# A state-space scan with routed experts: experts 4 to 7 in one wide pass, the first unit's scores first, and a copy moved to VectorE

## The chip, the cores and the metric

The kernel runs on one core of a Trainium2 chip. The time is device microseconds (us) of one launch, and a version is told by the median of several runs; the profile is of one further execution, whose own time is given beside its span. Engines are called by the names of the profile: PE is TensorE's matmul, PEld its weight load, DVE is VectorE, ACT ScalarE, POOL GpSimd, SP SyncE (here it only issues transfers).

## The reference

Two blocks, one after the other. The first is a state-space scan over 4 x 8 heads and 768 positions, in chunks; what it leaves is an array of 3072 tokens by 256. The second sends each token to one of eight experts, the one with the largest logit, and weighs what the expert gives by the softmax probability:

```python
y_intra = einsum('bhij,bhjd->bhid', CB * L, xc)
y_inter = einsum('bhin,bhnd->bhid', Cc, state) * decay_to_i
state = decay_full * state + sum(Bx)
...
logits = x @ w_gate                       # 3072 x 8
expert_idx = argmax(logits, axis=1)
for e in range(8):
    h = maximum(x[mask_e] @ w1[e], 0.0)   # 256 -> 1024
    out[mask_e] = gate_w[mask_e] * (h @ w2[e])
```

The inputs are fixed, and so is the routing: worked out from the reference, experts 0 to 7 get 372, 343, 418, 417, 336, 365, 415 and 406 tokens.

## The kernel before

**Scan.** Twelve steps `d` (L752 to L855), each for two units of 128 positions. For a unit `n`, `masked_C` (L254) makes two masked copies of C, `scores` (L274) multiplies them with B on PE into the accumulator `g`, `weigh` (L280) masks `g` into `M` on DVE, `scaled_x` (L264) divides x by its decay, `y_own` and `y_old` make the output on PE, ACT copies it (`turned`), and `rows` (L345) turns it and makes the logits. `totals` and `take_totals` (L243, L248) hand the decay over a whole chunk to the next one: `et` by DVE and `ew` by ACT, both read from the same PSUM bank that `rows` writes. Ahead of the loop (L731 to L746) stands the first pair of units by itself, with matmuls on zeros (`idle`) that keep PE at work.

**Places.** A token's place in the table `x_hbm` (an area of 3584 rows for each expert, in HBM) is its rank within its expert. GpSimd writes each unit's rows there by indirect transfers (`place`, L430). When all are placed, `over` (L447) works out where each expert's tokens end, and `empty_rest(e)` (L473) writes 128 empty rows behind the last token of expert `e`.

**Experts.** Everything is float32. `jobs` (L476) is the list of passes: sixteen before the change, (0, e) for the first 256 rows of each expert, then (1, e) for the rows from 256 on. A pass is
- `m_load(i)` (L479): SP issues four transfers of x into `xb`, one of logits and token numbers into `lt`, and, for the second pass of an even expert, two into `lh`.
- `m_xT(i)` (L515): DVE transposes `xb` to `xT`. For second passes it does so for two experts, i and i+1, and then for both `lt` and the `lh` runs `gates` (L498): three DVE operations, an exponential on ACT, three DVE operations.
- `m_h(i)` (L554): for each of eight blocks `f` two matmuls (`up`, L547) into one of four accumulators `h_ps`, then a relu by ACT into `hT`. After each block it calls `between(f)` of the loop at L869, which hands out other work. At f = 4 that is, in this order: weights of expert i+2 (`load_w`), `over` (i = 1), two `empty_rest` (i = 1 to 4), `m_load(i + 3)`, the switch number of a pair (`number_of`), and `m_xT(i + 1)`. So ACT gets the exponentials of `m_xT(i + 1)` ahead of its relus for f = 5, 6 and 7.
- `m_y(i)` (L581): for each tile of 128 rows eight matmuls into one of two accumulators `y_ps`, a scaling (`put`: by ACT, and by DVE from job 7 on) and an indirect transfer to the output on POOL's queue.

Second passes go in pairs of experts (`m_pair`, L615): a switch over 17 sizes, 128 to 192 rows in steps of 4, picks the code that fits the larger of the two counts; rows over 128 of both experts share one tile (`m_half`, L592). After pair k (L916) come `m_load` for pair k+2, `m_xT` for pair k+1, and `m_y` for both experts.

**Order.** The whole block is in `tc.manual_schedule()`: each engine and each queue runs its instructions in the order in which the code emits them, and waits are put in where data or buffers demand it. Reads and writes of `x_hbm` on SP's and POOL's queues wait for each other: a `m_load` for the `empty_rest` before it, an `empty_rest` for the `m_load` before it; only the indirect writes among themselves don't.

Of the kernel before, what the change touches and what calls it, by code (L numbers as in the profile page):

```python
# [9 lines left out]
FP32 = mybir.dt.float32  # L10
# [29 lines left out]
SLACK, FEW = 64, 64  # L40
NR = N + 512
EW = 3
# [5 lines left out]
def ssd_then_moe(ctx, tc, xs_in, ae_in, wgx, w_gate, w1, w2, gx, gb, gc, ga, out):  # L48
# [42 lines left out]
    steps = route.tile([1, len(SIZES) - 1], FP32, name="steps")  # L91
# [69 lines left out]
    def empty_consts():  # L161
        nc.gpsimd.memset(zrows, 0.0)
        none = sm.tile([128, 1], I32, name="none")
        nc.gpsimd.iota(none, pattern=[[0, 1]], base=N, channel_multiplier=0)
        nc.gpsimd.tensor_copy(zrows[:, TOK:TOK + 1].bitcast(I32), none)
        at_i = sm.tile([128, E], I32, name="at_i")
        nc.gpsimd.iota(at_i, pattern=[[NR, E]], base=0, channel_multiplier=1)
        nc.gpsimd.tensor_copy(at_r, at_i)
        steps_i = sm.tile([1, len(SIZES) - 1], I32, name="steps_i")
        nc.gpsimd.iota(steps_i, pattern=[[SIZES[1] - SIZES[0], len(SIZES) - 1]], base=P1 + SIZES[0],  # L170
                       channel_multiplier=0)
        nc.gpsimd.tensor_copy(steps, steps_i)
# [67 lines left out]
    def lasts(w):  # L240
        nc.vector.tensor_scalar(out=last[:, w], in0=here, scalar1=cum[:, w, CH - 1:CH], scalar2=None, op0=ALU.mult)  # L241
# [6 lines left out]
    def take_totals(w):  # L248
        p = r_ps[:, 1, 416:428]
        nc.vector.tensor_tensor(out=et[:, 12 * w:12 * w + 12], in0=bc(p[:, :, None], [128, 12, 2]),  # L250
                                in1=bc(par[:, None, :], [128, 12, 2]), op=ALU.mult)
        nc.scalar.copy(ew[:, 12 * w:12 * w + 12], p)  # L252

    def masked_C(n, dve=False):  # L254
        t = wk.tile([128, 2, CH], FP32, name="cm", bufs=4)
        for u in range(2):
            if dve:
                nc.vector.tensor_scalar(out=t[:, u], in0=st[n]["CT"], scalar1=par[:, u:u + 1], scalar2=None,
                                        op0=ALU.mult)
            else:  # L260
                nc.scalar.mul(t[:, u], st[n]["CT"], par[:, u:u + 1])  # L261
        st[n]["cm"] = t
# [184 lines left out]
    def over():  # L447
# [10 lines left out]
        nc.vector.tensor_tensor(out=over_, in0=bc(most[:, :, None], sh), in1=bc(steps[:, None, :], sh), op=ALU.is_gt)  # L458
# [17 lines left out]
    jobs = [(0, e) for e in range(E)] + [(1, e) for e in range(E)]  # L476
    ex = [dict() for _ in jobs]

    def m_load(i, engs=(nc.sync,)):  # L479

        p, e = jobs[i]
        r0, n = e * NR + P1 * p, (P1, P2)[p]
        xb = mo.tile([128, P1 // 32 * 64], FP32, name="xb", bufs=4)
        for c in range(4):
            engs[c % len(engs)].dma_start(out=xb[32 * c:32 * c + 32, 0:2 * n].rearrange("p (r z) -> p r z", z=64),
                              in_=x_hbm[r0:r0 + n, 64 * c:64 * c + 64].rearrange("(r j) z -> j r z", j=32))
        ex[i]["xb"] = xb[:, 0:2 * n].rearrange("p (r i k) -> p k r i", k=KT, i=32)
        lt = mo.tile([128, 2, MID], FP32, name="lt", bufs=7)[:, 0:2 - p]
        nc.sync.dma_start(out=lt, in_=x_hbm[r0:r0 + 128 * (2 - p), DM:W].rearrange("(t p) w -> p t w", p=128))
        ex[i]["lt"] = lt  # L490
        if p and e % 2 == 0:
            lh = mo.tile([128, 1, MID], FP32, name="lh", bufs=3)
            for u in range(2):
                q = r0 + u * NR + 128
                nc.sync.dma_start(out=lh[64 * u:64 * u + 64, 0], in_=x_hbm[q:q + 64, DM:W])
            ex[i]["lh"] = ex[i + 1]["lh"] = lh

    def gates(mid, n):  # L498

        sh = [128, n, E]  # L500
        l = mo.tile([128, 2, E], FP32, name="t_l", bufs=2)[:, 0:n]
        logits(l, mid)
        mx = mo.tile([128, 2], FP32, name="t_mx", bufs=2)[:, 0:n]
        nc.vector.tensor_reduce(mx, l, axis=AX, op=ALU.max)
        sub = mo.tile([128, 2, E], FP32, name="t_sub", bufs=2)[:, 0:n]
        nc.vector.tensor_tensor(out=sub, in0=l, in1=bc(mx[:, :, None], sh), op=ALU.subtract)
        nc.scalar.activation(sub, sub, func=ACT.Exp)  # L507
        se = mo.tile([128, 2], FP32, name="t_se", bufs=2)[:, 0:n]
        nc.vector.tensor_reduce(se, sub, axis=AX, op=ALU.add)  # L509
        nc.vector.tensor_scalar(out=se, in0=se, scalar1=1e-9, scalar2=None, op0=ALU.add)  # L510
        gt = mo.tile([128, 2], FP32, name="t_gt", bufs=8)[:, 0:n]
        nc.vector.reciprocal(gt, se)
        return gt

    def m_xT(i):  # L515
        p, e = jobs[i]
        n = (P1, P2)[p]
        for j in range(i, i + 1 + p):
            ex[j]["xT"] = mo.tile([128, KT, P1], FP32, name="xT", bufs=4)
            nc.vector.transpose(ex[j]["xT"][:, :, 0:n].rearrange("p k (r j) -> p k r j", j=32), ex[j]["xb"])  # L520
        if p:
            for j in range(i, i + 2):
                ex[j]["g"] = gates(ex[j]["lt"], 1)
# [3 lines left out]
    hT_all = [mo.tile([128, FT, P1], FP32, name=f"hT{k}") for k in range(3)]  # L527
# [26 lines left out]
    def m_h(i, pp, between):  # L554
        p, e = jobs[i]
        n = (P1, P2)[p]
# [24 lines left out]
    def m_y(i, pp, then=None):  # L581
        e = jobs[i][1]
        for t in range(2 - jobs[i][0]):
# [4 lines left out]
            put(p, ex[i]["lt"][:, t], ex[i]["g"][:, t:t + 1], i >= E - 1)  # L588
# [3 lines left out]
    def m_half(i, n, yo):  # L592
        e = jobs[i][1]
# [3 lines left out]
        p = y_next()  # L597
        for f in range(FT):
            for u in range(2):
                nc.tensor.matmul(p[64 * u:64 * u + n, :], lhsT=ex[i + u]["hT"][:, f, 128:128 + n],  # L600
                                 rhs=w_sb[e + u][1][:, f * DM:f * DM + DM], start=(f == 0), stop=(f == FT - 1))
        nc.scalar.mul(yo, p, ex[i]["gh"][:, 0:1])  # L602
# [12 lines left out]
    def m_pair(i, pp):  # L615

        e = jobs[i][1]
# [4 lines left out]
        for c in tc.Switch(chosen(e // 2), len(SIZES), hint=f"pair{e // 2}"):  # L622
            turn_no[:] = at
            n = SIZES[c]
# [4 lines left out]
            m_half(i, max(0, n - 128), yo)  # L629
# [84 lines left out]
    with tc.manual_schedule():  # L714
# [19 lines left out]
        idle(14)  # L734
        decays(0)
        masked_C(0)
        masked_C(1, dve=True)
        p0 = turn_decays(0)
        inverse(0, p0, 0, 4)
        for n in range(2):  # L740
            scores(n)
        rep_consts()
        scaled_x(0, nc.vector)
        scaled_x(1, nc.gpsimd)
        lasts(0)
# [6 lines left out]
        for d in range(ND):  # L752
# [37 lines left out]
            if d == 0:  # L790
                idle(3)
# [6 lines left out]
            weigh(2 * d)  # L798
            weigh(2 * d + 1)
            if d == 0:  # L800
                take_totals(0)
                inverse(0, p0, 4, 12)
# [37 lines left out]
            if d == 1:  # L840
# [3 lines left out]
                lasts(1)  # L844
# [16 lines left out]
        for e in range(EW, E):  # L861
            w_sb.append([w2pool.tile([128, KT * F], FP32, name=f"w{u + 1}_{e}") for u in range(2)])
        left = list(range(R0[LAST], NU))
# [5 lines left out]
        for i in range(E):  # L869
            def between(f):  # L870
# [21 lines left out]
                if EW <= i + 2 < E:  # L892
# [4 lines left out]
                if 1 <= i <= 4:  # L897
# [3 lines left out]
                if i == E - 1:  # L901
                    m_load(i + 4)
                if 2 <= i < 2 + E // 2:
                    number_of(i - 2)
                if i == E - 2:
# [6 lines left out]
            if i < E - 1:  # L912
                m_y(i, pp, (lambda: more_places(2)) if i == 0 else None)
        tc.switch_hint(chosen(0), len(SIZES), "pair0")
        m_y(E - 1, pp)
        for k in range(E // 2):  # L916
            i = E + 2 * k
            m_pair(i, pp)
            if k + 1 < E // 2:
                tc.switch_hint(chosen(k + 1), len(SIZES), f"pair{k + 1}")  # L920
                for u in range(4, 6):
                    if i + u < len(jobs):
                        m_load(i + u)
                m_xT(i + 2)
            m_y(i, pp)
            m_y(i + 1, pp)
    with tc.If(more[0] > 0):
# [65 lines left out]
```

## Time and profile before

| what | value |
|---|---|
| median of 3 runs | 248.17 us (247.75 to 251.34) |
| the profiled execution: its time | 247.47 us |
| the profiled execution: its span | 245.8 us |
| granted PE clock | 1.0 throughout |
| ACT busy | 92.7 us (38%) |
| POOL busy | 82.8 us (34%) |
| scan: PE, from the start to | 60.56 us |
| first passes, jobs 0 to 7, from / to | 60.56 / 172.95 us |
| second passes, from / to the last matmul's end | 172.95 / 240.9 us |

The span is the time from the first to the last instruction that the profiler recorded; 1.67 us lie around it. A float32 matmul stands in the records as two, so `up` of one expert makes 32 records of PE and a tile of `m_y` 16; these records are called passes of PE below. Busy times of PE are modelled at their ends, so the starts of successive stages say more than means.

### The profile page before, as it was taken

What the parts mean: (1) busy time and instruction counts of PE and PEld (TensorE: products, weight loads), DVE (VectorE), ACT (ScalarE), POOL (GpSimd) and SP (SyncE); (2) the same over time, 40 slices, a digit from 0 to 9 for tenths busy, and PEclk for the clock granted to TensorE, in tenths of its full rate; (3) what the DMA queues carried; (4) which work ended last, traced back from release to release, by engine and by line L of the source; (5) the groups of instructions that cost most, each with busy time, mean ns of one, the idle gap of its engine ahead of it and who ended that gap; (6) DMA issues with size and microseconds to landing.
All of it is one profiled execution on the core that took longest, in us unless ns stands there. A gap on an engine that the chain in (4) does not pass through costs nothing. (4 is left out here: it accounts for less than half of the span.)

```text
span 245.8 us, 5525 instructions
## 1 busy us (share of the span) xinstructions
PE 237.3 (97%) x2021; PEld 201.3 (82%) x2021; DVE 88.5 (36%) x279; ACT 92.7 (38%) x312; POOL 82.8 (34%) x144
## 2 busy tenths in 40 slices
PE   8889899999999999999999999999999999999992
PEld 5567778777888888888888888888999969989781
DVE  4699879998520222020201102052316007040000
ACT  4656768981322224141422324131432502614200
POOL 2484688880038506060413330111113012013031
PEclk9999999999999999999999999999999999999999
DMA  6999979965932278696867779454303100001001
GB/s 174 327 328 323 332 250 302 291 263 102 274 141 97 112 144 274 189 256 217 235 243 213 272 168 311 87 99 82 73 13 68 32 15 29 27 4 40 3 16 45
DMA packets 36407, 39.75 MB, mean 162 GB/s; under 512 B 21947, under 2 KB 23806, under 8 KB 36352
## 3 DMA queue, kind: packets, MB, share of 16 engines
q1 hardware_dynamic: 32816, 30.24, 43.2%
q0 software_dynamic: 2880, 8.66, 9.3%
q8 instruction: 27, 0.44, 0.7%
q10 hardware_dynamic: 656, 0.18, 0.3%
q14 instruction: 28, 0.23, 0.3%
HBM read 29.72 MB, written 9.86 MB: 161 GB/s over the span
## 5 line engine op out<-in xcount | busy, mean ns | idle before, releaser
L551 PE MATMUL h_ps<-xT,w 128*128 128x256 f32 (+3 forms) x512 | 90.0, 334 | 0.3 <-ACT hT L628 0.3
L551 PEld LDWEIGHTS h_ps<-xT,w 128*128 128x128 f32 x512 | 80.8, 190 | 7.6 <-ACT hT L628 0.7
L586 PE MATMUL y_ps<-w,hT 128*128 128x256 f32 x384 | 85.1, 380 | 0.0
L586 PEld LDWEIGHTS y_ps<-w,hT 128*128 128x128 f32 x384 | 72.6, 190 | 10.5 <-issue 0.8
L564 POOL DMA_INDIRECT out_dram<-yo,lt x24 | 23.8, 991 | 58.1 <-DVE yo L571 31.3
L509 DVE TENSOR_REDUCE t_se<-t_sub 128x1 f32<-128x8 f32 (+1 forms) x20 | 3.3, 165 | 102.8 <-ACT t_sub L507 102.8
L560 ACT ACTIVATE hT<-h_ps 128x256 f32<-128x256 f32 x64 | 24.4, 384 | 29.4 <-PE h_ps L551 28.9
L282 DVE TENSOR_TENSOR M<-g,mask 128x1024 f32<-128x1024 f32 x24 | 28.2, 1218 | 3.8 <-PE g L277 3.6
L628 ACT ACTIVATE hT<-h_ps 128x128 f32<-128x128 f32 (+2 forms) x64 | 18.0, 292 | 24.1 <-PE h_ps L551 24.1
L421 POOL DMA_INDIRECT x_hbm<-rows,pos x24 | 23.9, 994 | 9.3 <-DVE pos L408 5.3
L573 ACT ACTIVATE yo<-y_ps,t_gt 128x256 f32<-128x256 f32 x14 | 6.6, 474 | 43.2 <-PE y_ps L586 43.2
L421 POOL DMA_INDIRECT x_hbm<-zrows,rest x8 | 7.7, 962 | 35.4 <-DMA lt<-x_hbm 24.9
L335 PE MATMUL y<-M,xp 128*32 128x128 f32 x384 | 15.3, 277 | 1.6 <-DVE M L282 1.3
L347 PEld LDWEIGHTS r<-turn,yT 128*128 128x128 f32 x88 | 12.2, 189 | 4.4 <-ACT yT L340 3.0
L261 ACT ACTIVATE cm<-xs_n,par 128x128 f32<-128x128 f32 x46 | 15.1, 419 | 1.5 <-DMA xs_n<-in_xs_dram 1.5
L347 PE MATMUL r<-turn,yT 128*128 128x160 f32 x88 | 14.9, 312 | 0.7 <-ACT ew L252 0.7
L564 POOL DMA_INDIRECT out_dram<-yh,lh x4 | 3.9, 983 | 33.1 <-ACT yh L602 21.2
L277 PE MATMUL g<-cm,xs_n 32*128 32x256 f32 x192 | 15.0, 423 | 0.0
L271 POOL TENSOR_TENSOR xp<-xs_n,Ei 128x256 f32<-128x256 f32 x20 | 12.1, 617 | 6.8 <-DVE last L241 3.6
L571 DVE TENSOR_SCALAR yo<-y_ps,t_gt 128x256 f32<-128x256 f32 x10 | 4.7, 483 | 24.2 <-PE y_ps L586 24.2
L340 ACT COPY yT<-y 128x512 f32<-128x512 f32 x12 | 7.0, 586 | 16.1 <-PE y L335 14.2
L520 DVE STREAM_TRANSPOSE xT<-xb 128x512 f32<-128x512 f32 (+1 forms) x16 | 9.8, 632 | 8.6 <-DMA xb<-x_hbm 7.1
(123 smaller groups left out, 156.2 us busy)
## 6 DMA issues: line engine op xcount, KB each, us to landing
w<-in_w_dram SPq DMA_DIRECT2D x64, 256.0 KB, 5.8
xs_n<-in_xs_dram SPq DMA_DIRECT2D x20, 320.0 KB, 5.8
xb<-x_hbm SPq DMA_DIRECT2D x30, 64.0 KB, 2.3
xb<-x_hbm SPq DMA_DIRECT2D x32, 48.0 KB, 2.4
xs_n<-in_xs_dram SPq DMA_DIRECT2D x4, 192.0 KB, 3.6
x_hbm<-zrows SPq DMA_DIRECT2D x1, 672.0 KB
lt<-x_hbm SPq DMA_DIRECT2D x8, 80.0 KB, 2.7
xs_n<-in_xs_dram SPq DMA_DIRECT2D x4, 128.0 KB, 2.3
```

What stands on the lines that cost most here:

```text
L261: nc.scalar.mul(t[:, u], st[n]["CT"], par[:, u:u + 1])
L271: eng.tensor_tensor(out=t, in0=st[n]["x"].rearrange("p (h d) -> p h d", d=D), in1=bc(Ei[:, n, :, None], [128, NH, D]), op=ALU.mult)
L277: nc.tensor.matmul(g_ps[:, q, n % 2], lhsT=st[n]["BT"][r], rhs=st[n]["cm"][r].rearrange("p u i -> p (u i)"), start=True, stop=True)
L282: nc.vector.tensor_tensor(out=t, in0=g_ps[:, :, n % 2].rearrange("p q (u i) -> p q u i", u=2), in1=bc(mask[:, None, None, :], [128, 4, 2, ...
L335: nc.tensor.matmul(y_ps[o:o + D, h // 4, CH * s:CH * s + CH], lhsT=st[n]["xp"][:, D * h:D * h + D], rhs=st[n]["M"][:, h], start=first, sto ...
L347: nc.tensor.matmul((to[s] if to else r_ps[:, s])[:, 256 * t:256 * t + 160], lhsT=sd[d]["yT"][:, t, CH * s:CH * s + CH], rhs=turn[:, t].rea ...
L421: s_ = nc.gpsimd.indirect_dma_start(out=x_hbm[:, :], out_offset=bass.IndirectOffsetOnAxis(ap=at, axis=0), in_=row, in_offset=None)
L551: nc.tensor.matmul(p[:, 0:n], lhsT=w[:, c:c + 128], rhs=xT[:, t, 0:n], start=(t == 0), stop=(t == KT - 1))
L560: nc.scalar.activation(ex[i]["hT"][:, f, 0:n], q, func=ACT.Relu)
L564: return nc.gpsimd.indirect_dma_start(out=out[:, :], out_offset=bass.IndirectOffsetOnAxis(ap=tok, axis=0), in_=yo[:, :], in_offset=None, b ...
L586: nc.tensor.matmul(p, lhsT=ex[i]["hT"][:, f, 128 * t:128 * t + 128], rhs=w_sb[e][1][:, f * DM:f * DM + DM], start=(f == 0), stop=(f == FT ...
L628: nc.scalar.activation(ex[i + u]["hT"][:, f, 0:n], q, func=ACT.Relu)
```

## The change

1. **Start of the scan.** The first unit's masked C is made half by ACT and half by DVE, the second unit's wholly by ACT; the first unit's `scores` stand ahead of the turning of the decays on PE, its `weigh` ahead of the decays' inverse on DVE; three `idle` matmuls move in between the two units' scores. `lasts(0)` goes from DVE to GpSimd.
2. **Totals.** `take_totals` makes `ew` by DVE instead of ACT, and at d = 0 stands behind the second inverse.
3. **Experts.** Twelve jobs: (0, e) and (1, e) for experts 0 to 3, then (2, e) for experts 4 to 7, which takes all rows of an expert at once: 320 to 448 in steps of 8, three tiles of 128 in `m_y`, rows over 384 in `m_half`. The loop over first passes has 4 rounds, not 8. Three `hT` of 256 columns become two of 448, whose columns 320 to 383 are set to zero by GpSimd during the scan. Weights of experts 6 and 7 go into the buffers of experts 0 and 1 after pair 0. `empty_rest` of experts 0 to 5 stay in rounds 1 to 3, those of 6 and 7 go behind pair 0. `over` compares with two lists of sizes.

```diff
+HE = E // 2
+PASS = ((0, P1, 2), (P1, P2, 1), (0, P1 + P2, 3))
+WSIZES = list(range(P1 + FEW, P1 + P2 + 1, 8))
...
+        for hT in hT_all:
+            nc.gpsimd.memset(hT[:, :, WSIZES[0]:P1 + 128], 0.0)
...
-    def lasts(w):
-        nc.vector.tensor_scalar(out=last[:, w], in0=here, scalar1=cum[:, w, CH - 1:CH], scalar2=None, op0=ALU.mult)
+    def lasts(w, eng):
+        eng.tensor_scalar(out=last[:, w], in0=here, scalar1=cum[:, w, CH - 1:CH], scalar2=None, op0=ALU.mult)
...
-        nc.scalar.copy(ew[:, 12 * w:12 * w + 12], p)
+        nc.vector.tensor_copy(ew[:, 12 * w:12 * w + 12], p)
...
-    jobs = [(0, e) for e in range(E)] + [(1, e) for e in range(E)]
+    jobs = [(p, e) for p in range(2) for e in range(HE)] + [(2, e) for e in range(HE, E)]
...
-        r0, n = e * NR + P1 * p, (P1, P2)[p]
-        xb = mo.tile([128, P1 // 32 * 64], FP32, name="xb", bufs=4)
+        at, n, tiles = PASS[p]
+        r0 = e * NR + at
+        xb = mo.tile([128, (n if p == 2 else P1) // 32 * 64], FP32, name="xw" if p == 2 else "xb", bufs=2 if p == 2 else 4)
...
-        for j in range(i, i + 1 + p):
-            ex[j]["xT"] = mo.tile([128, KT, P1], FP32, name="xT", bufs=4)
+        for j in range(i, i + (2 if p else 1)):
+            ex[j]["xT"] = (mo.tile([128, KT, n], FP32, name="xTw", bufs=2) if p == 2 else
+                           mo.tile([128, KT, P1], FP32, name="xT", bufs=4))
...
-    hT_all = [mo.tile([128, FT, P1], FP32, name=f"hT{k}") for k in range(3)]
+    hT_all = [mo.tile([128, FT, P1 + P2], FP32, name=f"hT{k}") for k in range(2)]
...
-            n = SIZES[c]
+            n = (SIZES, WSIZES)[p - 1][c]
...
+        masked_C(0, (None, nc.vector))
+        masked_C(1)
         decays(0)
-        masked_C(0)
-        masked_C(1, dve=True)
+        scores(0)
         p0 = turn_decays(0)
+        idle(3, y_ps[:, 1, 256:512])
+        weigh(0)
+        scores(1)
         inverse(0, p0, 0, 4)
-        for n in range(2):
-            scores(n)
-        rep_consts()
         scaled_x(0, nc.vector)
         scaled_x(1, nc.gpsimd)
-        lasts(0)
+        rep_consts()
+        lasts(0, nc.gpsimd)
...
-        for i in range(E):
+        for i in range(HE):
...
-                if EW <= i + 2 < E:
+                if EW <= i + 2 < E - 2:
                     for k in range(8):
                         load_w(i + 2, *divmod(k, 4))
                 if i == 1:
                     over()
-                if 1 <= i <= 4:
+                if 1 <= i:
                     for e in range(2 * i - 2, 2 * i):
                         empty_rest(e)
                 m_load(i + 3)
-                if i == E - 1:
+                if i == HE - 1:
                     m_load(i + 4)
-                if 2 <= i < 2 + E // 2:
-                    number_of(i - 2)
+                if i >= 2:
+                    for k in range(2):
+                        number_of(2 * i - 4 + k)
...
                 m_xT(i + 1)
...
         for k in range(E // 2):
-            i = E + 2 * k
+            i = HE + 2 * k
             m_pair(i, pp)
             if k + 1 < E // 2:
...
+                m_xT(i + 2)
+                if k == 0:
+                    for e in range(E - 2, E):
+                        empty_rest(e)
                 for u in range(4, 6):
                     if i + u < len(jobs):
                         m_load(i + u)
-                m_xT(i + 2)
             m_y(i, pp)
             m_y(i + 1, pp)
+            if k == 0:
+                for e in range(E - 2, E):
+                    for j in range(8):
+                        load_w(e, *divmod(j, 4))
```

## The prediction

> **What bounds the kernel now.** I read the page's busy shares first, then PE's timeline, then the queues that feed it. The page's first lines:
>
> ```profile
> PE 237.3 (97%) x2021; PEld 201.3 (82%) x2021; DVE 88.5 (36%) x279; ACT 92.7 (38%) x312; POOL 82.8 (34%) x144
> ...
> L586 PE MATMUL y_ps<-w,hT 128*128 128x256 f32 x384 | 85.1, 380 | 0.0
> ```
>
> PE is busy 97%, and `m_y` waited 0.0 us: from 60.56 us on PE is the bound. Its timeline (start, length, what) shows how closely the stages follow each other. Round 3 of the first passes:
>
> ```profile
> 103.88 7.07 PE L551 MATMUL h_ps<-xT,w 128*128 128x256 f32 x32
> 110.79 7.07 PE L586 MATMUL y_ps<-w,hT 128*128 128x256 f32 x32
> 117.70 7.07 PE L551 MATMUL h_ps<-xT,w 128*128 128x256 f32 x32
> ```
>
> Start to start is 6.91 us for 32 passes, 215.9 ns each. But that no transfer is late holds only for this order of jobs. SP's timeline has the loads of jobs 4 and 5 (four `xb`, one `lt`) and between them the weights of expert 4:
>
> ```profile
> 100.86 1.81 SPq L485 DMA_DIRECT2D xb<-x_hbm  x4
> 102.71 0.45 SPq L489 DMA_DIRECT2D lt<-x_hbm  x1
> 103.21 3.81 SPq L204 DMA_DIRECT2D w<-in_w_dram  x8
> 114.01 1.81 SPq L485 DMA_DIRECT2D xb<-x_hbm  x4
> 115.86 0.45 SPq L489 DMA_DIRECT2D lt<-x_hbm  x1
> ```
>
> and POOL's has the empty rows that they wait for:
>
> ```profile
> 105.77 0.96 POOL L421 DMA_INDIRECT x_hbm<-zrows,rest  x1 [7.46 <-DMA lt<-x_hbm]
> ...
> 107.04 0.96 POOL L421 DMA_INDIRECT x_hbm<-zrows,rest  x1 [0.23 <-issue]
> ...
> 119.14 0.96 POOL L421 DMA_INDIRECT x_hbm<-zrows,rest  x1 [8.48 <-DMA lt<-x_hbm]
> ```
>
> This is a ring: `empty_rest` 2 and 3 wait until job 4's load has landed (105.77), job 5's load waits until they have landed (114.01, 6.97 us after the second was issued), and 119.14 tells when job 5 has landed. One turn takes 13.15 us (100.86 to 114.01), a round of PE 13.82. Before, nobody minds: job 5 was used at 131.5.
>
> What stands behind a late `m_xT` on ACT, from its timeline in round 7, the only round before that runs a pair's `m_xT`:
>
> ```profile
> 163.93 0.20 ACT L507 ACTIVATE t_sub<-t_sub 128x8 f32<-128x8 f32 x1
> 165.32 0.21 ACT L507 ACTIVATE t_sub<-t_sub 128x8 f32<-128x8 f32 x1 [1.18 <-DVE t_sub L506]
> 166.73 0.21 ACT L507 ACTIVATE t_sub<-t_sub 128x8 f32<-128x8 f32 x1 [1.21 <-DVE t_sub L506]
> 166.85 0.91 ACT L560 ACTIVATE hT<-h_ps 128x256 f32<-128x256 f32 x3
> ```
>
> The relus for f = 5, 6, 7 run only after the third exponential. PE had already begun `m_y(7)` at 166.04 and wanted f = 5 at 168.20.
>
> [...] 16 records of `scores` take 2.09 us at 4.62 and 1.15 at 9.83, though the granted clock shows 1.0. No long PE gap is in the trace. [...]
>
> **The change part by part.**
>
> *Start of the scan.* `weigh` of the first two units ran from 6.85 to 9.20, behind 16 cold records of `scores`, which were behind the turned decays. Now `scores(0)` can start at about 4.0 (masked C 3.36 + 0.42 on ACT and 0.27 on DVE; the `idle` row ends about then), ends after half of 2.09 at 5.1; DVE then does M (1.18), inverse 0.36, x 0.42, M 1.18: 8.4 to 8.5 against 9.20. `lasts` by GpSimd, nearest row 0.20 (TENSOR_SCALAR 128x8), lies behind x of unit 1; the three `idle` (0.49) lie in PE's wait for DVE. Bounds: gain 0.3 (if PE's own queue of own, totals, y sets the end) to 1.1 (scores warm). I take -0.6.
>
> *Totals.* At d = 4 PE's `rows` waited 0.67 at 30.15 for ACT's `ew`, which stood behind `state`. By DVE it is a copy of 0.17 (row `et`) at 28.13, in front of a DVE wait of 0.42 which hides it. Gain 0 to 0.7; POOL has 0.60, 0.28 and 0.21 of waits up to 50 us, so it can follow. I take -0.6.
>
> *GpSimd during the scan.* Two zero fills of 512 columns (`zrows`, 336 columns: 0.37; so 0.56 each) and one iota 0.13: 1.25, ahead of x of units 6 and 7 (16.32 to 17.5), which PE needs only at 22.1. POOL waits 2.60 at 20.11. 0; without that cover at most +1.2.
>
> *Wide passes.* [...] Counts 336/365 and 415/406 choose 368 and 416 (before 256+128 and 256+160). Before: four first passes 4 x 6.91 = 27.63, pair 2 from 206.78 to 213.92 = 7.14, pair 3 from 220.83 to 230.16 = 9.33; 44.10. After: 64 x 309.2 + 64 x 349.2 = 42.14, and 0.15 + 0.35 of entry to a case (7.14 - 64 x 0.1092; 9.06 - 64 x 0.1358): 42.64. -1.46; bounds -0.8 (only 16 columns x 64 x 0.83 ns) to -2. `m_y` and `m_half` keep their numbers (PE: 24 tiles, 64 half passes). A relu of 416 columns (0.31 at 164, 0.38 at 256, so about 0.51) hides behind four passes of 349; a transposition of 896 columns (0.54 at 384, 0.71 at 512, so 1.24) behind `m_y`. `over` gains one comparison on DVE (0.21 for 64, round 1), behind `rest`, which it doesn't delay. Two `hT` suffice: relus write a tile that PE's earlier `m_y` has left.
>
> *The moved second passes: the large term.* Job 4 is now the second pass of expert 0 and job 5 that of expert 1, loaded in rounds 1 and 2 as jobs 4 and 5 were, behind the same `empty_rest` 0, 1 and 2, 3. But now `m_xT(4)` in round 3 needs both, not 4 alone. In the old times (any gain of the scan shifts PE and the ring alike):
> - job 4: four `xb`, `lt`, two `lh`; the last is issued at about 103.7 instead of 102.71: +1.0 on `empty_rest` 2 and 3, whose second issue becomes 108.0.
> - job 5 is issued 6.97 later, at 115.0; its last `xb` at 116.4, landing 2.4 later (row `xb`, 48 KB): 118.8. A transposition of 384 columns behind it: 119.5.
> - first exponential 0.69 behind it (163.93 - 163.24, when DVE's pair of transpositions ended), the third 2.80 later, 0.20 long: 123.2; relu f = 5 by 123.6.
> - PE starts `m_y(3)` at 110.79, and has used f = 0 to 4 after ten passes, at 112.95.
>
> **PE stands from 112.95 to 123.6: +10.65.** Behind the waiting exponentials on ACT: relus 5 to 7, then the switch and relus of pair 0; behind the transposition on DVE: both `put` of `m_y(3)`, so both `y_ps`. Bounds: +8.3 (`empty_rest` lands 2 us sooner, the load smaller) to +12.7 (2 us later). [...]
>
> What is late next? On the delayed clock pair 1 starts at 144.1; jobs 6 and 7 are behind `empty_rest` 4, 5, weights of expert 5, and land by about 136.5, the exponentials end at 140.8, ACT's entry to a case of 164 rows takes 2.7 (186.27 to 188.95): 143.5. Covered by 0.6 and the four accumulators. Jobs 8 and 9 wait for `empty_rest` 6 and 7, which stand on POOL behind pair 0's output (about 138.9): landed at 147.5, twelve transfers to 153.5, `xT` 158, ACT ready about 165, PE's pair 2 at 163.9 with 5 us of accumulators. Covered. Weights of 6 and 7, 4 MB behind that on SP, are wanted only after 205.
>
> Sum on the profiled execution's span: 245.8 - 0.6 - 0.6 - 1.46 + 10.65 + 1.7 = 255.5; with the 1.67 around it 257.2. The median of the runs stands 0.70 above the profiled run's 247.47, so 257.9.
>
> **The rivals.** That the instructions don't move as the diff says is none: each queue's order is written out by hand.
> A. As above: 257.9; with its bounds (-2.3, +2.1 ring, -1.7, +1.7 cold, -1, +1.5 the gains, not all at once) 254.5 to 261.5.
> B. *Not slower:* job 5 lands in time. Then only the gains stay: 248.17 - 2.66 = 245.5. The point: the last `xb` landed by about 108.2 (112.95 less 4.8), and every microsecond beyond costs one; equal to before at 110.9. For it: the ring's 6.97 coincides with weights (2 MB), and the landing of `empty_rest` may owe much to them. Against it: the same weights are still there, and the load was issued at 114.01.
> C. *A second stall:* `empty_rest` 6, 7 or the twelve transfers take 5 us more than I took, and pair 2 or pair 1 waits too, with the strict queues: another 3 to 8, 263 at the middle.
> D. *The change of shape costs:* a pass over 256 columns takes 10% more than linear: 128 x 33 ns = +4.2, so 262. For it nothing; 128, 164 and 256 lie on one line.
>
> **The numbers.** A 0.80, B 0.10, C 0.07, D 0.03. 257.9 is A's. Faster or slower by 2% (4.96 us, about what a measurement of this kernel can tell from no change: 243.2 and 253.1) then: B is within 2%, mostly, and a thin part of A too; C and D are slower. Faster 0.03, same 0.11, slower 0.86. The range leaves out B and the far part of C; below it reaches to all of A's low ends at once (257.9 - 2.3 - 1.7 - 1 = 252.9), above to C's near half: 252.9 to 262.
>
> **What would show it.** In the changed kernel's PE timeline a gap of 8 to 13 us inside the fourth `m_y` of the experts, ended by ACT's `hT`, and in ACT's timeline the exponentials (L516) ahead of three relus, with the longest wait on DVE, and DVE's on `xb`. Right behind it passes of twice 216 ns for about 3 us. The scan's end about 1.2 earlier than 60.56; wide passes of 309 and 349 ns. Wrong I would be if job 5's load is issued before 110 or PE runs through that `m_y`.

## The result, and the profile after

The changed kernel takes **265.51 us** (median of 6 runs, 264.38 to 269.85) against 247.96 beside it: ratio **1.0692**, 95% interval 1.0658 to 1.0725. Slower, as forecast, but above the forecast's range. The profiled execution took 264.93 us with a span of 263.1; the sum had 255.5 for the span, so 7.6 us are missing. Some executions of a kernel are over 1.5% longer than its fastest; the ratios leave them out, and the profiles of e4 and e12 below are of such ones; only order and waits are read from them. The page's first lines, with the granted clock and the DMA engines' share in 40 slices, and the group of `m_y`:

```profile
PE 240.7 (91%) x1893; PEld 187.6 (71%) x1893; DVE 89.2 (34%) x260; ACT 82.9 (32%) x267; POOL 84.4 (32%) x148
...
PEclk9999999999999999985899999799999999999999
DMA  6998889948423694858631599970001100000011
...
L596 PE MATMUL y_ps<-w,hT 128*128 128x256 f32 x384 | 86.6, 385 | 10.9 <-ACT hT L570 10.4
```

PE falls from 97% to 91%. The 0.0 us that `m_y` waited are now 10.9. The clock row shows *two* dips, not one; the second stands above DMA digits of 9. PE's timeline (start, length, what; in brackets the idle time ahead and what ended it) shows both stops:

```profile
110.74 2.32 PE L596 MATMUL y_ps<-w,hT 128*128 128x256 f32 x10
123.48 6.56 PE L596 MATMUL y_ps<-w,hT 128*128 128x256 f32 x22 [10.42 <-ACT hT L570]
129.88 7.31 PE L561 MATMUL h_ps<-xT,w 128*128 128x128 f32 x64
...
156.89 7.17 PE L596 MATMUL y_ps<-w,hT 128*128 128x256 f32 x32
166.64 6.88 PE L561 MATMUL h_ps<-xTw,w 128*128 128x368 f32 x16 [2.57 <-DVE t_l L373]
174.75 15.11 PE L561 MATMUL h_ps<-xTw,w 128*128 128x368 f32 x48 [1.24 <-ACT hT L640]
189.69 7.07 PE L596 MATMUL y_ps<-w,hT 128*128 128x256 f32 x32
197.21 14.08 PE L596 MATMUL y_ps<-w,hT 128*128 128x256 f32 x64 [0.45 <-DVE yo L581]
211.13 22.51 PE L561 MATMUL h_ps<-xTw,w 128*128 128x416 f32 x64
```

The first stop is the predicted one: ten passes of `m_y(3)`, then idle to 123.48 (forecast 123.6). The second was not predicted: at pair 2's start PE is idle from about 164 to 166.64, does 16 passes in 6.88 (4.95 at the forecast's 309.2 ns; the granted clock was 0.5 from 167.6 to 171.0), and is idle again. Pair 2 takes 25.73 us from about 163.96, where `m_y` of pair 1 is done, to 189.69; 64 passes at 309.2 ns and 0.15 are 19.94. The bracket at 166.64 names DVE's `t_l`, which these matmuls don't read; their `xTw` was ready at 156.4, and the weight load ahead of them (PEld) waited 2.94 us for "issue". ACT's timeline tells the two stops apart:

```profile
120.14 0.21 ACT L516 ACTIVATE t_sub<-t_sub 128x8 f32<-128x8 f32 x1 [11.41 <-DVE t_sub L515]
121.53 0.21 ACT L516 ACTIVATE t_sub<-t_sub 128x8 f32<-128x8 f32 x1 [1.19 <-DVE t_sub L515]
122.95 0.21 ACT L516 ACTIVATE t_sub<-t_sub 128x8 f32<-128x8 f32 x1 [1.20 <-DVE t_sub L515]
123.06 0.91 ACT L570 ACTIVATE hT<-h_ps 128x256 f32<-128x256 f32 x3
...
157.04 0.48 ACT L614 ACTIVATE yh<-y_ps,t_gt 128x256 f32<-128x256 f32 x1 [3.31 <-PE y_ps L612]
163.90 0.22 ACT L516 ACTIVATE t_sub<-t_sub 128x24 f32<-128x24 f32 x1 [6.39 <-issue]
...
166.97 0.21 ACT L516 ACTIVATE t_sub<-t_sub 128x8 f32<-128x8 f32 x1 [1.24 <-DVE t_sub L515]
174.22 1.58 ACT L640 ACTIVATE hT<-h_ps 128x368 f32<-128x368 f32 x4 [7.04 <-PE h_ps L561]
```

At 120.14 ACT waits for *data*: `t_sub` is late because job 5's rows are. At 163.90 it waits for "issue", that is for nothing that the profile shows: DVE's transpositions ran at 151.53 and 155.05, and its `t_sub` was ready at 157.08. What stands there in the code is the end of one switch (leaving pair 1's case: ACT's "way out") and then, 7.04 us long, the beginning of the next (its "way in"; the four relus at 174.22 follow each other at once, so four accumulators stood full). In the kernel before, the ways out of pair 0 and into pair 1 took 2.38 and 2.68 us:

```profile
183.25 0.21 ACT L507 ACTIVATE t_sub<-t_sub 128x8 f32<-128x8 f32 x1 [2.38 <-issue]
...
188.95 0.91 ACT L628 ACTIVATE hT<-h_ps 128x164 f32<-128x164 f32 x4 [2.68 <-PE h_ps L551]
```

Third, the windows view: per stretch of 4 us the busy time of each engine, the clock, the DMA engines' share (which can come out above 1) and GB/s:

```profile
core 0: us, PE busy (x) PEld busy (x) DVE busy (x) ACT busy (x) POOL busy (x), PEclk, DMA share, GB/s
...
156.00:160.00 4.00, 4.00 (x24) 3.06 (x21) 1.02 (x4) 0.48 (x1) 0.98 (x1) 1.00 0.93 268
160.00:164.00 4.00, 4.00 (x19) 3.23 (x17) 0.00 (x0) 0.10 (x1) 0.00 (x0) 1.00 1.03 353
164.00:168.00 4.00, 1.43 (x5) 1.01 (x5) 2.82 (x16) 0.55 (x3) 0.00 (x0) 0.95 1.09 348
```

The DMA engines are full through both waits of ACT, but not with the same thing. SP's queue has the weights of experts 6 and 7 (4 MB, wanted only at 211) and behind them the rows of job 10, then of job 11:

```profile
152.77 11.26 SPq L209 DMA_DIRECT2D w<-in_w_dram  x16
164.24 2.56 SPq L494 DMA_DIRECT2D xw<-x_hbm  x4
```

and the packets of the transfers, over 157.5 to 164 and over 167.2 to 170.5, are

```profile
DMA packets 1155, 2.13 MB, mean 328 GB/s; under 512 B 151, under 2 KB 152, under 8 KB 1151
```

```profile
DMA packets 1632, 0.56 MB, mean 170 GB/s; under 512 B 1558, under 2 KB 1558, under 8 KB 1631
```

The way out lay beside the weights. The way in lay mostly beside the rows that the weights had held up on SP's queue: many small packets, few bytes.

### The profile page after: what moved, and what is told of

Its sections match the earlier page's. It is cut to its first block, busy times and chain, and to the rows that moved or that the text cites. A ratio compares the mean times of both kernels' runs of the same rounds, so it can differ in the third digit from the quotient of the medians.

```text
span 263.1 us, 5182 instructions
## 1 busy us (share of the span) xinstructions
PE 240.7 (91%) x1893; PEld 187.6 (71%) x1893; DVE 89.2 (34%) x260; ACT 82.9 (32%) x267; POOL 84.4 (32%) x148
## 5 line engine op out<-in xcount | busy, mean ns | idle before, releaser
L596 PE MATMUL y_ps<-w,hT 128*128 128x256 f32 x384 | 86.6, 385 | 10.9 <-ACT hT L570 10.4
L561 PE MATMUL h_ps<-xTw,w 128*128 128x368 f32 (+1 forms) x128 | 44.5, 509 | 3.8 <-DVE t_l L373 2.6
L561 PE MATMUL h_ps<-xT,w 128*128 128x256 f32 (+2 forms) x256 | 45.1, 335 | 0.1
L640 ACT ACTIVATE hT<-h_ps 128x128 f32<-128x128 f32 (+3 forms) x64 | 24.9, 396 | 60.5 <-PE h_ps L561 60.5
L561 PEld LDWEIGHTS h_ps<-xT,w 128*128 128x128 f32 x256 | 40.3, 190 | 3.7 <-DVE yo L581 0.5
L561 PEld LDWEIGHTS h_ps<-xTw,w 128*128 128x128 f32 x128 | 25.0, 197 | 22.6 <-issue 14.2
L581 DVE TENSOR_SCALAR yo<-y_ps,t_gt 128x256 f32<-128x256 f32 x18 | 8.5, 482 | 62.1 <-PE y_ps L596 62.1
L570 ACT ACTIVATE hT<-h_ps 128x256 f32<-128x256 f32 x32 | 12.1, 383 | 14.8 <-PE h_ps L561 14.2
L518 DVE TENSOR_REDUCE t_se<-t_sub 128x1 f32<-128x8 f32 (+2 forms) x16 | 2.7, 167 | 37.2 <-ACT t_sub L516 37.2
L530 DVE STREAM_TRANSPOSE xTw<-xw 128x896 f32<-128x896 f32 x4 | 4.7, 1176 | 29.6 <-PE h_ps L561 20.2
```

The lines of the kernel that those rows point to most:

```text
L561: nc.tensor.matmul(p[:, 0:n], lhsT=w[:, c:c + 128], rhs=xT[:, t, 0:n], start=(t == 0), stop=(t == KT - 1))
L570: nc.scalar.activation(ex[i]["hT"][:, f, 0:n], q, func=ACT.Relu)
L596: nc.tensor.matmul(p, lhsT=ex[i]["hT"][:, f, 128 * t:128 * t + 128], rhs=w_sb[e][1][:, f * DM:f * DM + DM], start=(f == 0), stop=(f == FT ...
L640: nc.scalar.activation(ex[i + u]["hT"][:, f, 0:n], q, func=ACT.Relu)
```

## The experiments

Each compares with the kernel before on its own chip; the ratio is the measure, and a distance to the changed kernel is the difference of the two ratios times 247.8 us.

**One part alone, on the kernel before.** e1 takes part 1 of the change, e2 part 2:

```diff
-        nc.scalar.copy(ew[:, 12 * w:12 * w + 12], p)
+        nc.vector.tensor_copy(ew[:, 12 * w:12 * w + 12], p)
```

> The kernel before with the change's part 1 alone (start of the scan). [...] scores of units 2 and 3 start at about 10.9 us instead of 9.83 and the whole is 1.0 us slower, about 249.0 against 248.0. Rival, the prediction's: the order gains 0.6 us as forecast and something else in the changed kernel (fills on GpSimd, later steps) took it back; then 247.4.

> The kernel before with the change's part 2 alone (ew by VectorE, behind the inverse at d = 0). Theory: rows at d = 4 no longer waits 0.67 us for ScalarE, the scan ends 0.7 us earlier: 247.3 against 248.0. Rival: the places on GpSimd's queue end the scan, nothing moves: 248.0.

e1: **1.0024** (0.9989 to 1.0059), 248.64 beside 247.79. Neither the forecast's gain (the interval reaches to -0.3 us, not to -0.6) nor a clear loss. e2: **0.9972** (0.9946 to 0.9998), some -0.7 us (forecast -0.6).

**e3: the weights of experts 6 and 7 later**, on the changed kernel:

```diff
-            if k == 0:
+            if k == 1:
                 for e in range(E - 2, E):
                     for j in range(8):
                         load_w(e, *divmod(j, 4))
```

> The changed kernel with the weights of experts 6 and 7 loaded behind pair 1 instead of pair 0. Theory, code behind weights: around pair 2 ScalarE stood 6.4 us with its data there and 7.0 us more until its first relu [...]; without them ScalarE enters pair 2 some 2.7 us behind its last exponential, the first exponential stands right behind yh, PE has no gap ahead of pair 2, and the whole is 5 to 6.5 us faster: about 259.5 against 265.5. Rival, late tables: the wide xw loads end it; VectorE's transpositions stay at 155 to 156, and the gain is under 1.5 us.

Measured 259.97, **1.0497** (1.0438 to 1.0556): 4.8 us off the changed kernel. The weights were issued from 160.09 instead of 152.77, and with them gone the rows of jobs 10 and 11 came from 151.69 instead of 164.24: the rows are ahead of the switch, and the weights begin behind ACT's way out. ACT's way out of pair 1 took 2.54 us, its way into pair 2 3.29. In PE's timeline the first stop is still there, the second is 0.88 us:

```profile
122.11 6.46 PE L596 MATMUL y_ps<-w,hT 128*128 128x256 f32 x22 [9.77 <-DMA w<-in_w_dram]
...
163.68 20.03 PE L561 MATMUL h_ps<-xTw,w 128*128 128x368 f32 x64 [0.88 <-DVE yo L581]
```

64 passes in 20.03 us also say that the wide pass costs what the forecast's price said, and that pair 2's rows had been in time.

**e4: the ring opened**, on the changed kernel: empty rows of experts 0 to 3 in round 1, both jobs behind them.

```diff
-                if 1 <= i:
-                    for e in range(2 * i - 2, 2 * i):
+                if i == 1:
+                    for e in range(4):
                         empty_rest(e)
-                m_load(i + 3)
-                if i == HE - 1:
+                if i == 3:
+                    for e in range(4, 6):
+                        empty_rest(e)
+                if i != 2:
+                    m_load(i + 3)
+                if i == 1 or i == HE - 1:
                     m_load(i + 4)
```

> The changed kernel with empty_rest 0 to 3 and the loads of jobs 4 and 5 all in round 1, so job 5's load waits for one landing of empty rows and not for a second turn of the ring. Theory, ring: job 5 is issued by 107 to 109 instead of 115.3, PE's stop of 10.4 us inside the fourth m_y falls to 0 to 3, and most of the 1.65 us of half-rate passes behind it goes too: 9 to 12 us faster, about 255. Rival, bandwidth: the load is late because weights fill the DMA engines, whatever it waits for; then it lands after 116 all the same and the gain is under 4 us.

Measured 255.66, **1.0292** (1.0216 to 1.0369): 9.9 us off. Job 5 was issued at 108.77 instead of 115.26, and the stop in `m_y(3)` shrank from 10.42 to 1.37 us. The second stop stayed: 2.93 and 1.49 us at pair 2, ACT's way out 5.86.

**e7: the order on ACT**, on the changed kernel: `m_xT(4)` behind the relus.

```diff
-                m_xT(i + 1)
+                if i < HE - 1:
+                    m_xT(i + 1)
             m_h(i, pp, between)
+            if i == HE - 1:
+                m_xT(HE)
```

> The changed kernel, with the transposition and exponentials of job 4 and 5 emitted behind all first passes and relus of round 3 instead of ahead of the last three relus. The rows land as late as before. Theory 'order on ACT': PE's long stop inside m_y(3) is made by three relus that stand behind exponentials in ACT's queue; now m_y(3) runs through, and the stop moves to pair 0, where PE has only four accumulators: it stops near 119.4 and goes on at 124.5 to 126 (the exponentials, then ACT's entry into the case), 5 to 7 us instead of 10.4 and a wait of 1 to 2 less of cold clock: 3 to 6 us faster than 265.5, so 259.5 to 262.5. Rival 'the rows' lateness alone counts': PE does the same work by the same landing, total within 1 us of 265.5.

Measured 262.11, **1.0559** (1.0494 to 1.0623): 3.3 us faster, inside the range of the theory. `m_y(3)` ran through, and PE stopped 5.23 us in pair 0 after 16 passes. So the order on ACT made about half of the 10.42 us of that stop, late rows the rest. The gain is smaller than that because another stop of 5.06 us came at pair 1, where ACT waited 8.03 us for `t_sub`.

**e5: weights' traffic alone**, on the kernel before: 4 MB that nobody needs, emitted behind pair 0. In this kernel they ran from 173.90 to 188.2, through pair 0 and into pair 1's start, not at pair 2 as expected.

```diff
             m_y(i + 1, pp)
+            if k == 0:
+                for e in range(2):
+                    for j in range(8):
+                        load_w(e, *divmod(j, 4))
```

> The kernel before, and behind its pair 0 the weights of experts 0 and 1 are loaded once more into the tiles that they already fill (16 transfers of 256 KB, the same 4 MB at the same place of SP's queue as the changed kernel's load of experts 6 and 7; nobody computes with them again). Nothing else changes: the passes, tables and rows of pair 2 are those of before. Theory 'entry behind weights': leaving one pair's case and entering the next costs ACT its 1.7 and 2.7 us only when the DMA engines are free; behind 4 MB both become 6 to 7 us, PE stops once or twice around the start of pair 2, +2 to +6 us, ratio 1.01 to 1.025, although everything that ACT reads is there. Rival 'rows late' or 'wide passes': in this kernel the rows of pair 2 are loaded far ahead, so 0 (ratio within 0.997 to 1.003).

Measured 249.66, **1.0061** (1.0036 to 1.0086): slower, but under the theory's 1.01. ACT's way out of pair 0 was 2.38 as before, its way into pair 1 3.46 instead of 2.68, PE's stop 0.58. The DMA share was 0.52 over 180 to 184 and 0.91 over 184 to 188: the way out lay beside half-empty engines. The way in did not, and yet was only 0.8 longer; the weights landed 4.5 us after their issue here (median), 6.5 in the changed kernel. The theory's direction, not its size.

**e6, e10, e11, e12: all repairs together**, the totals' copy and the wide passes kept, the start of the scan as before (except the first, each also has the weights of expert 3 in round 0):

- e6: e3's and e4's edits.
- e10: empty rows of 0 to 3 in round 1 and of 4 to 7 in round 2; jobs 4 and 5 in round 1, 6 in round 2, 7 in round 3; e3's edit.
- e11: jobs 6 and 7 in round 2 ahead of the empty rows of 4 to 7, which come in round 3; weights of 6 and 7 behind pair 0.
- e12: as e11, weights of 6 and 7 behind pair 1.

> The changed kernel with three parts taken back: the weights of experts 6 and 7 behind pair 1, the empty rows of experts 0 to 3 ahead of the loads of both jobs in round 1, and the start of the scan as before. What stays is the wide passes and the totals' copy. If the two stops explain all that the change lost: 265.5 less 9.9 less 5.5 and some tenths, so 249 to 250.5; if the wide passes also bring their -1.46 and the totals -0.7 with no third stop, 245.6 to 246.5, ratio 0.991 to 0.995. If wide passes cost more than they save, or a third stop follows, above 251.

> The changed kernel with wide passes and the totals' copy kept, the start of the scan as before, weights of expert 3 one round earlier and of experts 6 and 7 behind pair 1, empty rows of experts 0 to 3 in round 1 and 4 to 7 in round 2, and jobs 4 and 5 loaded in round 1, 6 in round 2, 7 in round 3: nothing of the ring is waited for. Sum on the kernel before: 247.8 - 1.46 (wide) - 0.7 (totals) = 245.6; range 245 to 246.8, ratio 0.989 to 0.996. Rival 'a third stop' (transfers of weights and rows closer together, code for the cases behind them): 248 or more.

> The changed kernel with wide passes and the totals' copy kept and the start of the scan as before; every row of a later pass is loaded as soon as it can be: the weights of expert 3 in round 0, empty rows of experts 0 to 3 and jobs 4 and 5 in round 1, jobs 6 and 7 and the weights of expert 4 in round 2 with no empty rows ahead of them, the weights of expert 5 and then the empty rows of experts 4 to 7 in round 3, jobs 8 and 9 and the weights of experts 6 and 7 behind pair 0 as in the changed kernel. If only the ring and the DMA engines' load at a pair's start made the changed kernel slow, nothing is left to wait for at m_y(3), pair 1 and pair 2: 247.8 - 1.46 (wide) - 0.7 (totals) = 245.6, range 245 to 247. The weights of 6 and 7 now start about 130, when pair 1 is entered; if PE or ACT is stopped there, they take 2 to 4 us more: 248 to 250. Rival, that wide passes or the changed order cost by themselves: above 250 with no stop over 1 us in PE's timeline.

> The kernel of e11_rows_first, with one thing moved: the weights of experts 6 and 7 (4 MB) behind pair 1 instead of pair 0. All rows are as early as there. Theory 'code behind data': a pair's exit and entry on ACT and PE last as long as the DMA engines leave room; where the engines' mean share in the trace is 0.9 or more beside an entry it takes 5 to 7 us and PE stops 2 to 5 us, where the share is under 0.6 it takes 2.2 to 3. If the weights start at pair 2's entry (about 145 to 150), this kernel is 2 to 5 us slower than e11_rows_first; if they start behind it, equal or up to 3 us faster, as pair 1's entry is then free. Rival 'rows late': both the same within 0.5 us, as the rows are in time in both.

None reaches the kernel before: **1.0163** (1.0102 to 1.0224), **1.0483** (1.0427 to 1.0540), **1.0247** (1.0181 to 1.0314) and **1.0295** (1.0238 to 1.0352). Each time the stop at `m_y(3)` was gone or small, and another had come. In e6 and e10 it was pair 1, whose rows (jobs 6 and 7) now came late behind weights or behind the empty rows: ACT waited 4.70 and 11.37 us for DVE's `t_sub`. e11's PE timeline has it at pair 0, with all rows in time:

```profile
123.46 2.84 PE L561 MATMUL h_ps<-xT,w 128*128 128x128 f32 x24
128.13 0.80 PE L561 MATMUL h_ps<-xT,w 128*128 128x128 f32 x4 [1.83 <-issue]
129.59 7.07 PE L561 MATMUL h_ps<-xT,w 128*128 128x128 f32 x36 [0.66 <-ACT hT L640]
```

There SP issued 4 MB of weights of experts 4 and 5 from 117.86 to 130. ACT had entered pair 0 at 124.11 and stood 2.97 us after its second relu, until 127.80; PE had long filled the accumulator, and no packet of the two queues of the kind "instruction" began there between 123.62 and 133.36. This stop's cause stays open; e12 has a wait of 4.01 us at the same place. The order of e11 and e12 is the theory's, but their intervals overlap, so the two together decide nothing.

**e9: the start of the scan as before**, on the changed kernel, the reverse of e1's edit.

> The changed kernel with the start of the scan as before. The prediction's -0.6 for that part: this kernel 0.6 us slower than the changed one (266.1). What the changed kernel's profile shows, scores and own rows at half rate there (+1.0 us): 0.5 to 1 us faster (264.5 to 265). Neither, as with that part alone on the kernel before (1.0024 of before): within 0.5 us of 265.5.

**1.0617** (1.0560 to 1.0673), on a chip where the kernel before took 254.99. It overlaps the changed kernel's interval: with e1, no gain of part 1 is shown.

**e13 and e14: the weights spread.** e13 is e11 with the weights of experts 4 and 5 in round 1 and those of 6 and 7 held back until pair 2's relus are done; e14 leaves that last thing out and issues them behind pair 1 (`k == 1`, after its `m_y`), so that they run at pair 2's start. e13's added lines:

```diff
+                if i == 1 and f == 1:
+                    for k in range(8):
+                        load_w(HE, *divmod(k, 4))
...
                     m_load(HE + 1)
+                    for k in range(8):
+                        load_w(HE + 1, *divmod(k, 4))
...
             m_pair(i, pp)
+            if k == 2:
+                nc.gpsimd.tensor_copy(w_sb[E - 2][0][0:1, 0:1], ex[i + 1]["hT"][0:1, 0, 0:1])
+                for e in range(E - 2, E):
+                    for j in range(8):
+                        load_w(e, *divmod(j, 4))
```

> The kernel of e11_rows_first with the weights spread: those of experts 4 and 5 already in round 1 (one ahead of the rows of jobs 2 and 3, one behind those of job 5), those of experts 6 and 7 only when pair 2's relus are done (a copy of one element by GpSimd, 128 columns long at no engine that bounds, holds them back). From round 3 to pair 2 only rows move. Theory 'code behind data': with the DMA engines' share under 0.8 beside every pair's exit and entry, ACT's exits take 2.2 to 3, its entries 2.5 to 3.5, and PE has no stop over 1 us from its first pass of expert 0 to the end: ratio to before 0.988 to 0.998 (-1.46 for wide passes, -0.7 for the totals, up to +1 for small waits). Rival 'wide passes or the new order cost by themselves', or a stop that has another cause: 1.01 or more.

> As e13_spread, with one thing changed: the weights of experts 6 and 7 (4 MB) are not held back but stand behind the rows of jobs 10 and 11, so that they start about 145 to 152, beside pair 2's exit and entry. Every row that pair 2 needs is in place before them. Theory 'code behind data': ACT's exit before pair 2, its entry into it, or PE's, grows from some 2.5 to 4 to 7 us, PE stops 2 to 5 us there, ratio 0.01 to 0.02 above e13_spread. Rival 'rows late': no difference (within 0.003).

e13: **0.9942** (0.9911 to 0.9972), 245.94 beside 247.69: 0.6% faster than the kernel before, the only one of the combined kernels that is. That is 1.4 us of the 2.2 that wide passes and totals were to give. e14: **1.0012** (0.9981 to 1.0043), 0.0070 or 1.7 us slower than e13 on the same chip; the intervals don't touch, though the gap is under the 0.01 expected. e13's PE timeline has no stop over 0.6 us:

```profile
110.80 7.09 PE L596 MATMUL y_ps<-w,hT 128*128 128x256 f32 x32
117.73 7.31 PE L561 MATMUL h_ps<-xT,w 128*128 128x128 f32 x64
124.87 7.07 PE L596 MATMUL y_ps<-w,hT 128*128 128x256 f32 x32
132.54 9.17 PE L561 MATMUL h_ps<-xT,w 128*128 128x164 f32 x64 [0.60 <-DVE yo L581]
...
152.24 20.02 PE L561 MATMUL h_ps<-xTw,w 128*128 128x368 f32 x64
```

e14's has one, ahead of pair 2:

```profile
155.00 20.02 PE L561 MATMUL h_ps<-xTw,w 128*128 128x368 f32 x64 [1.87 <-DVE yo L581]
```

The weights on SP, the last exponential before pair 2 and the first relu in it on ACT, first in e13, then in e14:

```profile
174.53 11.70 SPq L209 DMA_DIRECT2D w<-in_w_dram  x16
151.52 0.21 ACT L516 ACTIVATE t_sub<-t_sub 128x8 f32<-128x8 f32 x1 [1.24 <-DVE t_sub L515]
154.29 0.48 ACT L640 ACTIVATE hT<-h_ps 128x368 f32<-128x368 f32 x1 [2.56 <-PE h_ps L561]
```

```profile
148.04 11.33 SPq L209 DMA_DIRECT2D w<-in_w_dram  x16
152.44 0.21 ACT L516 ACTIVATE t_sub<-t_sub 128x8 f32<-128x8 f32 x1 [1.24 <-DVE t_sub L515]
158.62 1.22 ACT L640 ACTIVATE hT<-h_ps 128x368 f32<-128x368 f32 x3 [5.97 <-PE h_ps L561]
```

And the windows of e13 and e14 there:

```profile
148.00:152.00 4.00, 4.00 (x20) 3.53 (x19) 2.30 (x14) 0.66 (x3) 0.00 (x0) 1.00 0.20 53
152.00:156.00 4.00, 4.00 (x14) 2.39 (x13) 1.07 (x4) 0.95 (x2) 1.97 (x2) 1.00 0.18 59
```

```profile
148.00:152.00 4.00, 4.00 (x20) 3.53 (x19) 1.78 (x11) 0.45 (x2) 0.00 (x0) 1.00 0.94 254
152.00:156.00 4.00, 2.13 (x9) 1.33 (x8) 1.58 (x7) 0.21 (x1) 1.79 (x2) 1.00 0.93 289
```

In both, exponentials and data are ready at the same place in the order, and the rows of jobs 10 and 11 are issued before 148. What differs is that the weights start at 148.04 in e14 and at 174.53 in e13 (and a copy of one element on GpSimd there). With the DMA share at 0.93 instead of 0.19, ACT's way into the case takes 5.97 us instead of 2.56. That alone would have cost PE nothing: its four accumulators last for 16 passes, to about 159.96, and the relus begin at 158.62. PE's 1.87 us lie ahead of its first pass, so PE's own way into the case is late too.

## Why the prediction was right in direction and wrong in size

- **The ring: right.** Job 5 issued at 115.26 (forecast 115.0), its transposition at 118.97 (118.8), the third exponential ended at 123.16 (123.2), PE idle 10.42 us (10.65). e4 shows the cause by taking it away, e7 the share of the order on ACT (about half).
- **Slow passes behind the stop: right.** 22 passes took 6.40 us, from 123.48 to 129.88, where 22 x 0.2159 are 4.75: 1.65 more (1.7). The granted clock was 0.5 from 116.41 to 126.65; up to there the starts lie 426 to 588 ns apart, behind it 216. The sum's 1.7 was the author's estimate, and nothing in the profile before showed it: PE has no such stop there, and PEclk is 9 in all 40 slices.
- **Wide passes: right.** The 309.2 and 349.2 ns of the forecast were the author's estimate; the trace before bears them out. Start to start (median) a pass takes 136 ns there at 160 columns, 139 at 164 and 216 at 256, and the line through 160 and 256 comes to 309 at 368 and 349 at 416. (128 columns take 112, not the 109.2 in the forecast's entry to a case.) In the changed kernel 48 passes of 368 columns took 14.94 (174.75 to 189.69): 311 ns, forecast 309.2; 416 columns 22.44 / 64 = 351 ns (349.2). Rival D falls. In e13 pair 2's and pair 3's passes take 19.86 and 22.44, 42.30 against the 42.64 forecast.
- **Totals: right in size.** The masking steps that ran 0.91 us later than before ahead of d = 4's totals ran 0.18 later behind them: 0.73 gained (0.6), and e2 has 0.7.
- **Start of the scan, -0.6: wrong.** The scan ended at 60.61, before at 60.56, with the totals' gain inside. In the profiled execution the second unit's scores and both units' own rows ran slowly (8 scores in 1.24 us, 0.71 in e1; 32 own rows in 1.72, 1.08 in e1), so `scores` of units 2 and 3 began 1.04 later than before; in e1's profile they began 0.10 earlier. Part of this is chance: the first record of the granted clock, of 1.0, begins at 10.59 us here, at 7.07 before and 5.79 in e1 (5.61 in e3, whose start is the changed kernel's), and the view shows 1.0 ahead of that as well. The 16 slow `scores` that the prediction's -0.6 rests on were such a chance too: e2, with the same start, ran them in 1.21 us, not 2.09. Even e1's profile has a tenth of a microsecond, not 0.6. Of the 7.6 us missing, 1.2 are this term and the totals together.
- **"What is late next?": the step that failed.** It put the first `m_xT` of pair 2 and ACT's entry together from rows and engine times, found ACT ready at 165 with five microseconds of accumulators, wrote "Covered", and dismissed the weights of experts 6 and 7 as "wanted only after 205". When they are wanted is one question; what else is moving while they move is the other. Its rows were in time, as it said (155.05 for the second transposition). But its price for entering a case, 2.7 us, had been read where the DMA engines' share was 0.43 (186.27 to 188.95), and it had no price for the way out, 2.38 at a share of 0.02. Here the 4 MB, and the rows behind them, kept the share at 1.00 and 1.07: 6.39 + 7.04. For PE that is 5.8 us (25.73 - 19.94), half-rate passes included. Rival C had the right place and nearly the right end (263), with another mechanism: rows that land late.
- **`m_y(8)`: a term left out.** 0.7 us are lost there, where DVE takes the larger gates of the next pair before the scalings. It is no cost of the weights: e13 loses 0.66 at the same place, the kernel before nothing.

The sum with these in place of the forecast's: 255.5 + 1.3 up to pair 2's start (start and totals together brought nothing: 60.61 against 60.56) + 5.8 + 0.7 - 0.3 (pair 3's passes, 22.44 against 22.70) = 263.0; the span is 263.1.

**What is shown, and what is argued.** Shown, by e13 against e14: 4 MB of weights beside a switch make ACT's way in 3.4 us longer and PE's late by 1.9, although all data is there. Starting them later, and with that the rows of jobs 10 and 11 earlier, took 3.9 us off the way out and 3.8 off the way in (e3 against the changed kernel). That it is the *code* of the case that comes late is not shown; it is argued from the packets of two queues. The page of the changed kernel lists two DMA queues of the kind "instruction": q8 carried 27 packets of 0.44 MB in all, 16 KB each, q14 29 of 0.24 MB, 8 KB each. The time at which each packet began stands in the traces:

| | wait began | packet began | engine went on | after the packet |
|---|---|---|---|---|
| ACT, way in, e13 | 151.73 | q14 152.61 | 154.29 | 1.68 |
| ACT, way in, e14 | 152.65 | q14 156.97 | 158.62 | 1.65 |
| ACT, way out, changed kernel | 157.51 | q14 161.89 | 163.90 | 2.01 |
| ACT, way in, changed kernel | 167.18 | q14 172.12 | 174.22 | 2.10 |
| PE, into pair 2, e13 | none | q8 149.55 | 152.24 | 2.69 |
| PE, into pair 2, e14 | 153.13 | q8 152.34 | 155.00 | 2.66 |
| PE, into pair 2, changed kernel | 164.07 | q8 163.85 | 166.64 | 2.79 |

All of the difference between e13 and e14 lies ahead of the packet. (PE's packet begins before its wait, while it still works off the matmuls ahead.) The other runs agree: the eleven stops of PE over 0.8 us ahead of a pair's first pass all ended 2.66 to 2.93 us after a packet of q8 began. The eleven waits of ACT over 5 us around pair 2 ended 1.35 to 2.44 us after one of q14 began; in the five waits over 2 us at the switches of the kernel before it was 1.74 to 2.21. That q8 brings PE's code and q14 ACT's is inferred from these intervals; the trace names no engine. Why a packet begins late beside other traffic is not shown: the late ones of q14 above took 0.31 us in e14 and at the way out, no longer than others. The kernels already announce each next case (`switch_hint`); a kernel without it, or with a case's code in place earlier, was not tried. Nor is e12 against e11 settled, nor why e5's traffic cost only 1.5 us.

## What to carry to other kernels

Before calling a stage covered, ask not only when a transfer is wanted but what moves beside it: in a program with switches like this one, bulk loads belong where no engine changes its case (ACT's way in took 2.56 us in e13 and 5.97 beside the weights in e14), and a load that is not urgent can be held back by a data dependence, as e13 does. Making a stage's rows earlier by moving others moved the stop here, until weights, empty rows and rows were laid out over the whole stretch: e6, e10, e11 and e12 each had another stop in place of the first. A transfer that is late by one stage costs more than its lateness when an engine's order has other work behind the wait for it (e7: about half of the 10.42 us).

## What the runs showed of the hardware

- Leaving one case of a switch and entering the next cost ACT 2.2 to 2.6 us each in e13, where the DMA engines' share over the wait was up to 0.62, and 4.6 to 7.0 us in the twelve longest waits around pair 2, with it at 0.82 to 1.14. The share alone doesn't set the price: e5's way in took 3.46 us at 0.93. That this price depends on other traffic had not been expected.
- How long PE's records at the scan's start run slowly differs from one execution to the next: the same 16 `scores` took 2.09 us in the profile of the kernel before and 1.21 in e2's. The record of the granted clock begins at 7.07 and 4.69 us there, and the view shows 1.0 ahead of it too; an arrangement of that stretch can't be judged by one profile.
- After PE's stop of 10.42 us the granted clock was 0.5 until 126.65, 3.2 us after PE went on. After the stop of 2.57 us it was 0.5 from 167.6 to 171.0; after 2.62 us in e10 and 2.32 in e9, at the same place, it stayed at 1.0.
- One chip took 254.99 us for the kernel before, where the others took 247.7 to 248.0; only ratios to runs on the same chip are compared above.
